# Sums, logits and rows of a pair of heads moved between the score steps of the next pair

## The chip, the cores and the metric

The kernel runs on one core of one Trainium2 chip. The time is the device time of one execution, in microseconds (us); lower is better. The core has five engines that run their own instruction streams in order and meet at semaphores: PE (TensorE; PEld is its weight loads), ACT (ScalarE), DVE (VectorE), POOL (GpSimd) and SP (SyncE, which here only issues DMAs).

## The reference

Two stages. Attention over 4 batches, 8 heads, 768 positions, 64 values per head, in which each query sees only the six best of 24 chunks of keys; then a layer of 8 experts, which takes at most 80 tokens per expert.

```python
k_min, k_max = min and max of k over each chunk of 32 keys
ub = sum over d of maximum(q * k_min, q * k_max), causal by chunk
sel = the 6 chunks with the largest ub, for each query
scores = where(sel & causal, q @ k.T / 8, -1e9)
attn_out = softmax(scores) @ v

x = attn_out as (3072, 512)
logits = x @ w_gate
expert = argmax(logits);  gate = softmax(logits)[expert]
for e in range(8):
    tok = the tokens of expert e; if more than 80, the 80 with the largest gate
    out[tok] = gate[tok] * (relu(x[tok] @ w1[e]) @ w2[e])      # all other rows are 0
```

## The kernel before

A helper, `op(engine, function, r=..., w=...)`, records every operation with what it reads and writes and puts the semaphore waits. Each engine runs its operations in the order in which the program emits them, so the order of the calls below is the order on each engine, and an operation that waits holds up all that its engine has behind it.

Two heads make a pair; 16 pairs (`NP`), four to a batch (`NPB`), are run one after the other. For pair i the loop emits:

- `scores(i)`: six steps. In each, matmuls of keys against queries (L498) and mask matmuls (L504, from `unsT`) fill one of two score tiles `SC[0]`, `SC[1]` in turn; ACT takes the exponential into `EXB` (L509); POOL clears the part above the diagonal (L514, a select) and adds what is there into `ES` (L523, the fold). `ES` becomes the sum over key tiles, from which the softmax's denominators come.
- in the first pair of a batch, `gate`, `gate_digits` and `gate_T` of the batch before: gate values from the logits (DVE, with one exponential on ACT at L586), their transposes on PE into `OB` (L599), and a copy by ACT into the row of candidates `cand` (L601).
- `bounds(i + 1)`: the upper bounds of the next pair (PE into `M0` and `MB`, L463; then DVE to the mask `uns`, L479).
- `transposes(i + 2)`: q and k of the pair after that through `SC[0]` and `SC[1]` (L425), copied out by ACT (qT, rq) and by DVE (kT, and its minima and maxima per chunk); POOL subtracts (L441).
- `load(i + 4)`: q and k by SP.
- `values(i)`: the value products (L534) into `OB`, copied by ACT to `oT` (L538). Then v of pair i + 2 is loaded.
- `unselT(i + 1)`: transposes of the mask (L485) and ACT's copy to `unsT` (L487).
- `wload`: one megabyte of an expert's weights, issued by POOL.
- `rows(i)`: six transposes of `oT` into `OB` (L559).
- `sums(i)`: into `M0`, the pair's part of the logits (`oT` by the gate weights, L544), then the denominators (`ES` by ones, L549); DVE turns them (L552) and takes reciprocals.
- `scale_rows(i)`: DVE scales the rows into `xp` (L567) and the logits into `lgp` (L571), and SP stores `xp` to memory (L573).
- `rounds(i, ..)`: between these, ten rounds per batch (three in each of the first three pairs of the next batch, one in the fourth), each a maximum of 8 over `cand` and a replacement (L620, L622), which find the 80 best tokens of each expert.

After the last pair come the gate of the last batch, its ten rounds, the slots of the tokens, and the experts.

Of the kernel before, what the change touches and what calls it, by code (L numbers as in the profile page):

```python
# [5 lines left out]
ACTF = mybir.ActivationFunctionType  # L6
# [141 lines left out]
def bass_quest_chunk_select__then__topk_capacity_drop_kernel(  # L148
# [10 lines left out]
    B, H, S, D = q.shape  # L159
    E = moe_w_gate.shape[1]  # L160
    Fd = moe_w1.shape[2]
    Dm = moe_w_gate.shape[0]
    CAP = int(moe_capacity)
    NT = S // 128
# [4 lines left out]
    NPB = H // 2  # L169
    NP = B * NPB  # L170
# [4 lines left out]
    def ts(i, n=128):  # L175
        return bass.ts(i, n)
# [27 lines left out]
    with ExitStack() as pers:  # L204
# [16 lines left out]
        op = sy.op  # L221

        with nc.Block() as blk:

            @blk.sync
            def _body(_unused):
# [259 lines left out]
                           r=["uns", "ident_bf"], w=["MB"], inc=(t == NT - 2))  # L486
                    op("act", lambda: ac.activation(unsT[j][:], MB[:, 0:(NT - 1) * 128], ACTF.Copy), r=["MB"], w=[f"unsT{j}"])  # L487

                def scores(i):
                    j = i % 2  # L490
                    for st, pieces in enumerate(STEPS):
                        s = st % 2
                        for pi, (kt, q0, q1, c) in enumerate(pieces):
                            last = pi == len(pieces) - 1
                            for h in range(2):
                                pr = slice(h * 64, h * 64 + 64)
                                o = SC[s][:, h * 512 + c:h * 512 + c + q1 - q0]
                                op("pe", lambda: pe.matmul(o, kT[j][pr, ts(kt)], qT[j][pr, q0:q1], start=True, stop=False),  # L498
                                   r=[f"kT{j}", f"qT{j}"], w=[f"SC{s}"], inc=False)
                            b0 = max(q0, 128)  # L500
                            for h in range(2):
                                pr = slice(h * 64, h * 64 + 64)
                                o = SC[s][:, h * 512 + c + b0 - q0:h * 512 + c + q1 - q0]
                                op("pe", lambda: pe.matmul(o, ind[pr, ts(kt)], unsT[j][pr, b0 - 128:q1 - 128],  # L504
                                                           start=False, stop=True),
                                   r=[f"ind{h}", f"unsT{j}"], w=[f"SC{s}"], inc=last)
                        W = pieces[-1][3] + pieces[-1][2] - pieces[-1][1]
                        src = bass.AP(SC[s], 0, [[1024, 128], [512, 2], [1, W]])
                        op("act", lambda: ac.activation(Ex(st, None, 0, W), src, ACTF.Exp, scale=SCALE),  # L509
                           r=[f"SC{s}"], w=[f"E{st}"])  # L510
                        d = DIAG[st]
                        a = Ex(st, None, d, 128)
                        ad, ak = (ES[:, :, 0:128], "ES0") if st == 0 else (a, f"E{st}")
                        op("gp", lambda: gp.affine_select(ad, a, pattern=[[0, 2], [1, 128]], compare_op=ALU.is_ge, fill=0.0,  # L514
                                                          base=0, channel_multiplier=-1), r=[f"E{st}"], w=[ak])
                        for (s2, c2, q0, q1) in ADDS[st]:
                            n = q1 - q0
                            o = ES[:, :, q0:q1]
                            in1 = Ex(s2, None, c2, n)
                            first = FIRST.get((s2, c2))  # L520
                            in0 = Ex(first[0], None, first[1], n) if first else o
                            kt = [f"ES{t}" for t in range(q0 // 128, q1 // 128)]
                            op("gp", lambda: gp.tensor_tensor(o, in0, in1, ALU.add),  # L523
                               r=[f"E{s2}", f"E{first[0]}"] if first else [f"E{s2}"] + kt, w=kt)
# [32 lines left out]
                def rows(i):  # L557
                    for t in range(NT):
                        op("pe", lambda: pe.transpose(OB[:, ts(t)], oT[:, ts(t)], ident_f[:]),  # L559
                           r=["oT0", "oT1", "ident_f"], w=[f"O{t // 4}"], inc=(t in (3, NT - 1)))  # L560
# [12 lines left out]
                    op("sp", lambda: sp.dma_start(xdst, xp[:]), r=["xp"], w=[f"xd{i}"],  # L573
                       dsem=f"d_xd")

                def gate(b):
                    j0 = b * NT

                    def along(t, n=NT):
                        return bass.AP(t, 0, [[n, 128], [1, n], [0, E]])  # L580

                    op("dve", lambda: ve.tensor_reduce(lg[:], lgp[:], AX, ALU.add),
                       r=[f"lgp{p}" for p in range(NPB)], w=["lg"])
                    op("dve", lambda: ve.tensor_reduce(lmax[:], lg[:], AX, ALU.max), r=["lg"], w=["lmax"])
                    op("dve", lambda: ve.tensor_tensor(lg[:], lg[:], along(lmax), ALU.subtract), r=["lg", "lmax"], w=["lg"])
                    op("act", lambda: ac.activation(lgx[:], lg[:], ACTF.Exp), r=["lg"], w=["lgx"])  # L586
                    op("dve", lambda: ve.scalar_tensor_tensor(oh[:], lg[:], 0.0, rank_c[:], ALU.is_ge, ALU.mult),
                       r=["lg", "rank_c"], w=["oh"])
                    op("dve", lambda: ve.tensor_reduce(lmax[:], oh[:], AX, ALU.max), r=["oh", "lmax"], w=["lmax"])
                    op("dve", lambda: ve.tensor_reduce(lsum[:], lgx[:], AX, ALU.add), r=["lgx"], w=["lsum"])  # L590
                    op("dve", lambda: ve.tensor_tensor(oh[:], oh[:], along(lmax), ALU.is_equal), r=["oh", "lmax"], w=["oh"])
                    op("dve", lambda: ve.tensor_scalar(lsum[:], lsum[:], 1e-9, None, ALU.add), r=["lsum"], w=["lsum"])
                    op("dve", lambda: ve.reciprocal(gt6[:], lsum[:]), r=["lsum"], w=["gt6"])
                    op("dve", lambda: ve.tensor_tensor(gv[:, j0:j0 + NT, :], oh[:], along(gt6), ALU.mult),  # L594
                       r=["oh", "gt6"], w=[f"gv{b}"])

                def gate_T(b):
                    for t in range(NT):
                        op("pe", lambda: pe.transpose(OB[0:E, ts(t)], gv[:, b * NT + t, :], ident_f[:]),  # L599
                           r=[f"gv{b}", "ident_f"], w=["O0" if t < 4 else "O1"], inc=(t in (3, NT - 1)))  # L600
                    op("act", lambda: ac.activation(cand[:, CAP:CAP + S], OB[0:E, 0:S], ACTF.Copy), r=["O0", "O1"], w=["cand"])  # L601

                def gate_digits(b):

# [22 lines left out]

                ROUNDS = CAP // 8

                def rounds(i, lo, hi):  # L630

                    if i < NPB:
                        return
                    for n in range(lo, hi):
                        m = (i % NPB) * 3 + n
                        if m < ROUNDS:
                            top_round(m, False)

                def warm(n):
                    for _ in range(n):  # L640
# [17 lines left out]
                    pr = slice(h * 64, h * 64 + 64)  # L658
                    op("dve", lambda: ve.tensor_copy(wg[pr, :, h * E:(h + 1) * E], wgr[pr, :, :]), r=["wg", f"wgr{h}"], w=[f"wg{h}"])
                for i in range(NP):  # L660
                    scores(i)
                    if i % NPB == 0 and i:
                        gate(i // NPB - 1)
                        gate_digits(i // NPB - 1)
                    if i % NPB == 0 and i:
                        gate_T(i // NPB - 1)
                    if i + 1 < NP:
                        bounds(i + 1)
                    if i + 2 < NP:
                        transposes(i + 2)  # L670
                    if i + 4 < NP:
                        load(i + 4, "qk")
                    rounds(i, 0, 1)
                    values(i)
                    if i + 2 < NP:
                        load(i + 2, "v")
                    if i + 1 < NP:
                        unselT(i + 1)
                    rounds(i, 1, 2)
                    if i < NP - 1:  # L680
                        wload(i // 2, i % 2)
                    rows(i)
                    sums(i)
                    scale_rows(i)
                    rounds(i, 2, 3)
                    if i % 3 == 2 and i < 12:
                        zk = f"w1_{E - 1}"
                        zr = bass.AP(w1s[E - 1], 0, [[DB * Fd, 128], [1, 2 * Dm]])
                        if i == 2:
                            op("dve", lambda: ve.memset(zr, 0.0), w=[zk])  # L690
                        g = i // 3
                        zs = bass.AP(w1s[E - 1], 0, [[DB * Fd, 128], [0, NT], [1, 2 * Dm]]).bitcast(F32)
                        zd = bass.AP(out.tensor, out.offset + g * NT * 128 * Dm, [[Dm, 128], [128 * Dm, NT], [1, Dm]])
                        op("sp", lambda: sp.dma_start(zd, zs), r=[zk], w=[f"outz{g}"], dsem=f"d_zero{g}")


                b = B - 1
                gate(b)
                gate_T(b)
                gate_digits(b)  # L700
# [152 lines left out]
```

## Time and profile before

| | |
|---|---|
| time, median of 3 runs | 373.32 us (371.21 to 375.81) |
| time of the profiled execution | 370.24 us |
| its span, first to last instruction | 368.5 us |
| PE busy | 297.6 us, 81% |
| POOL busy | 231.8 us, 63% |
| DVE busy | 231.2 us, 63% |
| ACT busy | 149.3 us, 41% |
| granted TensorE clock, mean | 0.915 |

Busy time is summed over a span that has different stages: 16 pairs of heads up to about 295 us, then some 40 us in which DVE is nearly alone, then the experts. What an engine's share means has to be read from one stage. Ends of matmuls are modelled. The granted clock is a share of 2.4 GHz.

### The profile page before, as it was taken

How to read it: one execution, taken by the hardware profiler on the slowest of the kernel's cores; microseconds unless marked ns; L12 is line 12 of the kernel's file. 1: busy time of each engine (PE TensorE's matmuls, PEld its weight loads, DVE VectorE, ACT ScalarE, POOL GpSimd, SP SyncE). 2: the span in 40 equal slices, each digit the busy share in tenths (PEclk: the TensorE clock that was granted, in tenths of full speed). 3: DMA queues.
4: the chain of work that ended last, by engine and by line, in shares of the span. 5: the costliest groups of instructions: out<-in, count | busy, mean ns of one | idle time of the engine just before them, and what ended most of it. 6: DMA issues, size and time to landing. Idle time of an engine off the chain costs nothing.

```text
span 368.5 us, 7857 instructions
## 1 busy us (share of the span) xinstructions
PE 297.6 (81%) x3244; PEld 183.4 (50%) x3244; DVE 231.2 (63%) x591; ACT 149.3 (41%) x202; POOL 231.8 (63%) x313
## 2 busy tenths in 40 slices
PE   6599999997899999969999999699989610034993
PEld 6255656463656465536556564456454400024771
DVE  3734425254987696759896963896866079881442
ACT  3273645545345536353736455345535110002320
POOL 5077869696739696785778696919696940006422
PEclk9699999999899999999999999899999855555999
DMA  9937889899495999786989778763638090001211
GB/s 175 193 67 137 159 143 177 138 299 171 91 156 114 143 305 165 143 126 129 265 189 181 136 156 131 221 104 77 114 67 133 4 135 1 0 2 42 59 55 53
DMA packets 104964, 47.50 MB, mean 129 GB/s; under 512 B 88955, under 2 KB 97269, under 8 KB 104928
## 3 DMA queue, kind: packets, MB, share of 16 engines
q1 hardware_dynamic: 89920, 27.94, 32.5%
q0 software_dynamic: 13440, 18.67, 31.8%
q10 hardware_dynamic: 1568, 0.39, 0.6%
q8 instruction: 25, 0.41, 0.4%
q14 instruction: 11, 0.09, 0.1%
HBM read 53.10 MB, written 10.75 MB: 173 GB/s over the span
## 4 chain that ended last, share of the span: by engine, by line
POOL 40%; PE 34%; issue 12%; ACT 7%; DVE 4%; DMA 1%; POOLq 0%
POOL ES L523 32%; PE SC L498 10%; ACT EXB L509 7%; POOL EXB L514 6%; PE OB L534 5%; PE OB L797 4%; PE M L549 4%; PE SC L782 3%; PE SC L504 2%; PE SC L425 2%; PE M L463 1%; PE OB L559 1%; DVE gv L594 1%; DMA kn<-x_rows,idx 1%; PE OB L599 1%
## 5 line engine op out<-in xcount | busy, mean ns | idle before, releaser
L509 ACT ACTIVATE EXB<-SC 128x1024 f32<-128x1024 f32 x96 | 86.3, 916 | 60.9 <-PE SC L504 58.9
L523 POOL TENSOR_TENSOR ES<-ES,EXB 128x256 f32<-128x256 f32 (+1 forms) x112 | 106.8, 965 | 6.4
L498 PE MATMUL SC<-qT,kT 64*128 64x512 f32 (+3 forms) x512 | 98.0, 471 | 1.8
L534 PE MATMUL OB<-EXB,vn 128*64 128x256 f32 (+2 forms) x704 | 71.9, 360 | 0.0
L498 PEld LDWEIGHTS SC<-qT,kT 64*128 64x128 f32 x512 | 40.9, 188 | 42.4 <-ACT EXB L509 26.4
L534 PEld LDWEIGHTS OB<-EXB,vn 128*64 128x64 f32 x704 | 46.7, 137 | 23.0 <-issue 10.0
L523 POOL TENSOR_TENSOR ES<-EXB 128x768 f32<-128x768 f32 (+1 forms) x32 | 49.3, 1541 | 1.3
L620 DVE MAX8 top<-cand 8x8 f32<-8x848 f32 (+1 forms) x40 | 40.2, 1006 | 1.9 <-ACT cand L601 1.3
L504 PE MATMUL SC<-unsT,ind 64*128 64x384 bf16 (+3 forms) x256 | 38.9, 297 | 0.0
L514 POOL TENSOR_SCALAR_AFFINE_SELECT EXB<-EXB 128x256 f32<-128x256 f32 x80 | 31.0, 407 | 10.7 <-ACT EXB L509 10.7
L538 ACT ACTIVATE oT<-OB 128x512 f32<-128x512 f32 (+1 forms) x32 | 15.7, 490 | 53.5 <-PE OB L534 53.5
L622 DVE MATCH_REPLACE8 cand<-top,cand 8x848 f32<-8x848 f32 (+1 forms) x36 | 35.7, 992 | 0.0
L467 DVE STREAM_TRANSPOSE M<-M 128x160 f32<-128x160 f32 x16 | 5.8, 363 | 46.3 <-PE MB L463 46.3
L514 POOL TENSOR_SCALAR_AFFINE_SELECT ES<-EXB 128x256 f32<-128x256 f32 x16 | 6.4, 400 | 43.2 <-ACT EXB L509 43.2
L552 DVE STREAM_TRANSPOSE M<-M 128x192 f32<-128x192 f32 x16 | 6.3, 393 | 35.8 <-PE M L549 35.8
L763 POOL DMA_INDIRECT qn<-x_rows,idx x4 | 3.9, 980 | 35.4 <-issue 35.4
L504 PEld LDWEIGHTS SC<-unsT,ind 64*128 64x128 bf16 x256 | 13.0, 95 | 14.4 <-issue 11.1
L430 ACT ACTIVATE qT<-SC 128x768 f32<-128x768 f32 x16 | 13.0, 811 | 17.2 <-PE SC L425 17.2
L549 PE MATMUL M<-ES,onc 128*32 128x192 f32 x256 | 14.3, 343 | 5.0 <-POOL ES L523 4.3
L774 ACT ACTIVATE rq<-MB 128x320 bf16<-128x320 bf16 x4 | 1.7, 437 | 39.5 <-PE MB L771 39.5
L425 PE MATMUL SC<-ident_f,qn 128*128 128x128 f32 x96 | 15.1, 298 | 3.1 <-ACT EXB L509 1.4
L714 PE MATMUL M<-dg,ones 8*128 8x8 f32 x2 | 0.6, 367 | 20.9 <-DVE dg L712 20.9
(141 smaller groups left out, 449.8 us busy)
## 6 DMA issues: line engine op xcount, KB each, us to landing
w1s<-in_moe_w_dram POOLq DMA_DIRECT2D x8, 1024.0 KB, 9.6
w2s<-in_moe_w_dram POOLq DMA_DIRECT2D x7, 1024.0 KB, 10.3
qn<-in_q_dram SPq DMA_DIRECT2D x32, 192.0 KB, 4.0
vn<-in_v_dram SPq DMA_DIRECT2D x32, 192.0 KB, 3.1
out_dram<-w1s SPq DMA_DIRECT2D x4, 1536.0 KB, 11.5
kn<-in_k_dram SPq DMA_DIRECT2D x30, 192.0 KB, 4.1
x_rows<-xp SPq DMA_DIRECT2D x16, 192.0 KB, 7.5
EXB<-in_moe_w_dram POOLq DMA_DIRECT2D x1, 1024.0 KB, 9.9
```

The lines of the kernel that those rows point to most:

```text
L425: op("pe", lambda: pe.transpose(SC[ps][:, ts(t)], a, ident_f[:]), r=[f"{nm}{s}0", f"{nm}{s}1", "ident_f"], w=[f"SC{ps}"], inc=(t == NT - 1))
L498: op("pe", lambda: pe.matmul(o, kT[j][pr, ts(kt)], qT[j][pr, q0:q1], start=True, stop=False), r=[f"kT{j}", f"qT{j}"], w=[f"SC{s}"], inc=False)
L504: op("pe", lambda: pe.matmul(o, ind[pr, ts(kt)], unsT[j][pr, b0 - 128:q1 - 128], start=False, stop=True), r=[f"ind{h}", f"unsT{j}"], w=[f" ...
L509: op("act", lambda: ac.activation(Ex(st, None, 0, W), src, ACTF.Exp, scale=SCALE), r=[f"SC{s}"], w=[f"E{st}"])
L514: op("gp", lambda: gp.affine_select(ad, a, pattern=[[0, 2], [1, 128]], compare_op=ALU.is_ge, fill=0.0, base=0, channel_multiplier=-1), r=[ ...
L523: op("gp", lambda: gp.tensor_tensor(o, in0, in1, ALU.add), r=[f"E{s2}", f"E{first[0]}"] if first else [f"E{s2}"] + kt, w=kt)
L534: op("pe", lambda: pe.matmul(OB[pr, q0:q1], vn[s][:, kt, h, :], ex, start=(n == 0), stop=last), r=[f"vn{s}{h}", "ES0" if st is None else f ...
L538: op("act", lambda: ac.activation(oT[:, q0:q1], OB[:, q0:q1], ACTF.Copy), r=[f"O{bk}"], w=[f"oT{bk}"])
L549: op("pe", lambda: pe.matmul(M0[c * 32:c * 32 + 32, 0:192], onc[:, h, :], stripes(ES, h * S + c * 32, 0, 0, None), start=False, stop=(h == ...
L620: op("dve", lambda: ve.max(dst, cv), r=["cand"], w=[f"top{int(last)}{n}"])
L622: op("dve", lambda: ve.match_replace(cv, dst, cv, -2.0), r=["cand", f"top{int(last)}{n}"], w=["cand"])
L797: op("pe", lambda: pe.matmul(o, hTv(e)[:, fb * CAP:(fb + 1) * CAP], w2v(e)[:, fb, :], start=(fb == 0), stop=(fb == FB - 1)), r=[f"hT{s}{fb ...
```

## The change

`scores` is split by a range of steps, and the selects and folds of steps 0 and 1 become a function of their own, `folds`. In pair i, steps 0 and 1 come first, then `sums(i - 1)`, then the folds of steps 0 and 1, steps 2 and 3, `rows(i - 1)` and `scale_rows(i - 1)`, and steps 4 and 5. The gate is cut in two: `gate_in` (logits summed, less their maximum, and the exponential) comes after the scores and ahead of `bounds(i + 1)`; the rest and `gate_digits` after it. `gate_T` writes `SC[0]` in place of `OB` and comes after `unselT`. The rounds shift: in the first pair of a batch one at its end, in the other three pairs three each. After the last pair `sums`, `rows` and `scale_rows` of that pair are emitted before the gate.

```diff
--- before.py
+++ after.py
@@ -486,9 +486,9 @@
                            r=["uns", "ident_bf"], w=["MB"], inc=(t == NT - 2))
                     op("act", lambda: ac.activation(unsT[j][:], MB[:, 0:(NT - 1) * 128], ACTF.Copy), r=["MB"], w=[f"unsT{j}"])
 
-                def scores(i):
+                def scores(i, lo, hi):
                     j = i % 2
-                    for st, pieces in enumerate(STEPS):
+                    for st, pieces in list(enumerate(STEPS))[lo:hi]:
                         s = st % 2
                         for pi, (kt, q0, q1, c) in enumerate(pieces):
                             last = pi == len(pieces) - 1
@@ -508,6 +508,11 @@
                         src = bass.AP(SC[s], 0, [[1024, 128], [512, 2], [1, W]])
                         op("act", lambda: ac.activation(Ex(st, None, 0, W), src, ACTF.Exp, scale=SCALE),
                            r=[f"SC{s}"], w=[f"E{st}"])
+                        if lo:
+                            folds(st)
+
+                def folds(*sts):
+                    for st in sts:
                         d = DIAG[st]
                         a = Ex(st, None, d, 128)
                         ad, ak = (ES[:, :, 0:128], "ES0") if st == 0 else (a, f"E{st}")
@@ -573,17 +578,18 @@
                     op("sp", lambda: sp.dma_start(xdst, xp[:]), r=["xp"], w=[f"xd{i}"],
                        dsem=f"d_xd")
 
-                def gate(b):
-                    j0 = b * NT
-
-                    def along(t, n=NT):
-                        return bass.AP(t, 0, [[n, 128], [1, n], [0, E]])
-
+                def along(t, n=NT):
+                    return bass.AP(t, 0, [[n, 128], [1, n], [0, E]])
+
+                def gate_in(b):
                     op("dve", lambda: ve.tensor_reduce(lg[:], lgp[:], AX, ALU.add),
                        r=[f"lgp{p}" for p in range(NPB)], w=["lg"])
                     op("dve", lambda: ve.tensor_reduce(lmax[:], lg[:], AX, ALU.max), r=["lg"], w=["lmax"])
                     op("dve", lambda: ve.tensor_tensor(lg[:], lg[:], along(lmax), ALU.subtract), r=["lg", "lmax"], w=["lg"])
                     op("act", lambda: ac.activation(lgx[:], lg[:], ACTF.Exp), r=["lg"], w=["lgx"])
+
+                def gate(b):
+                    j0 = b * NT
                     op("dve", lambda: ve.scalar_tensor_tensor(oh[:], lg[:], 0.0, rank_c[:], ALU.is_ge, ALU.mult),
                        r=["lg", "rank_c"], w=["oh"])
                     op("dve", lambda: ve.tensor_reduce(lmax[:], oh[:], AX, ALU.max), r=["oh", "lmax"], w=["lmax"])
@@ -596,9 +602,9 @@
 
                 def gate_T(b):
                     for t in range(NT):
-                        op("pe", lambda: pe.transpose(OB[0:E, ts(t)], gv[:, b * NT + t, :], ident_f[:]),
-                           r=[f"gv{b}", "ident_f"], w=["O0" if t < 4 else "O1"], inc=(t in (3, NT - 1)))
-                    op("act", lambda: ac.activation(cand[:, CAP:CAP + S], OB[0:E, 0:S], ACTF.Copy), r=["O0", "O1"], w=["cand"])
+                        op("pe", lambda: pe.transpose(SC[0][0:E, ts(t)], gv[:, b * NT + t, :], ident_f[:]),
+                           r=[f"gv{b}", "ident_f"], w=["SC0"], inc=(t == NT - 1))
+                    op("act", lambda: ac.activation(cand[:, CAP:CAP + S], SC[0][0:E, 0:S], ACTF.Copy), r=["SC0"], w=["cand"])
 
                 def gate_digits(b):
 
@@ -627,14 +633,14 @@
 
                 ROUNDS = CAP // 8
 
-                def rounds(i, lo, hi):
+                def rounds(i, m):
 
                     if i < NPB:
                         return
-                    for n in range(lo, hi):
-                        m = (i % NPB) * 3 + n
-                        if m < ROUNDS:
-                            top_round(m, False)
+                    k = i % NPB
+                    n = 0 if m == 2 and k == 0 else 3 * k - 2 + m
+                    if k or m == 2:
+                        top_round(n, False)
 
                 def warm(n):
                     for _ in range(n):
@@ -658,31 +664,39 @@
                     pr = slice(h * 64, h * 64 + 64)
                     op("dve", lambda: ve.tensor_copy(wg[pr, :, h * E:(h + 1) * E], wgr[pr, :, :]), r=["wg", f"wgr{h}"], w=[f"wg{h}"])
                 for i in range(NP):
-                    scores(i)
-                    if i % NPB == 0 and i:
+                    scores(i, 0, 2)
+                    if i:
+                        sums(i - 1)
+                    folds(0, 1)
+                    scores(i, 2, 4)
+                    if i:
+                        rows(i - 1)
+                        scale_rows(i - 1)
+                    scores(i, 4, 6)
+                    first = i % NPB == 0 and i > 0
+                    if first:
+                        gate_in(i // NPB - 1)
+                    if i + 1 < NP:
+                        bounds(i + 1)
+                    if first:
                         gate(i // NPB - 1)
                         gate_digits(i // NPB - 1)
-                    if i % NPB == 0 and i:
-                        gate_T(i // NPB - 1)
-                    if i + 1 < NP:
-                        bounds(i + 1)
                     if i + 2 < NP:
                         transposes(i + 2)
                     if i + 4 < NP:
                         load(i + 4, "qk")
-                    rounds(i, 0, 1)
+                    rounds(i, 0)
                     values(i)
                     if i + 2 < NP:
                         load(i + 2, "v")
                     if i + 1 < NP:
                         unselT(i + 1)
-                    rounds(i, 1, 2)
+                    if first:
+                        gate_T(i // NPB - 1)
+                    rounds(i, 1)
                     if i < NP - 1:
                         wload(i // 2, i % 2)
-                    rows(i)
-                    sums(i)
-                    scale_rows(i)
-                    rounds(i, 2, 3)
+                    rounds(i, 2)
                     if i % 3 == 2 and i < 12:
                         zk = f"w1_{E - 1}"
                         zr = bass.AP(w1s[E - 1], 0, [[DB * Fd, 128], [1, 2 * Dm]])
@@ -695,6 +709,10 @@
 
 
                 b = B - 1
+                sums(NP - 1)
+                rows(NP - 1)
+                scale_rows(NP - 1)
+                gate_in(b)
                 gate(b)
                 gate_T(b)
                 gate_digits(b)
```

## Rows read from the trace of the kernel before

**Rows 1.** Windows cut at pairs' first score matmuls: length, then busy us (instructions) per engine.
```profile
core 0: us, PE busy (x) PEld busy (x) DVE busy (x) ACT busy (x) POOL busy (x), PEclk, DMA share, GB/s
16.80:34.36 17.56, 17.17 (x176) 10.01 (x175) 7.09 (x22) 9.26 (x12) 13.01 (x18) 0.93 0.53 114
...
83.53:105.20 21.67, 18.08 (x186) 11.41 (x182) 16.82 (x44) 9.48 (x13) 13.21 (x18) 0.92 0.72 118
105.20:121.58 16.38, 15.89 (x180) 9.49 (x176) 12.95 (x32) 8.55 (x11) 12.78 (x17) 1.00 0.77 159
...
154.37:174.43 20.06, 16.46 (x185) 10.03 (x182) 15.26 (x42) 9.48 (x13) 13.26 (x18) 1.00 0.67 118
...
223.58:245.20 21.62, 18.02 (x185) 11.26 (x181) 16.77 (x44) 9.48 (x13) 13.24 (x18) 0.92 0.70 144
...
277.95:295.08 17.13, 14.02 (x130) 7.63 (x126) 5.53 (x11) 6.37 (x8) 13.47 (x19) 0.92 0.45 74
```
**Rows 2.** The chain that ended last, one pair: start us, length us, work.
```profile
107.63 1.03 ACT EXB L509
109.21 1.81 POOL ES L523
...
120.79 0.86 PE M L549 x16
```
**Rows 3.** Timeline of one plain pair: start, length, engine, line, [idle before <-releaser].
```profile
107.18 0.38 PE L504 MATMUL SC<-unsT,ind 64*128 64x512 bf16 x2
...
107.63 1.13 PE L498 MATMUL SC<-qT,kT 64*128 64x512 f32 x4
...
108.59 0.38 PE L504 MATMUL SC<-unsT,ind 64*128 64x512 bf16 x2
...
108.81 0.60 PE L498 MATMUL SC<-qT,kT 64*128 64x256 f32 x4
...
109.78 0.28 PE L504 MATMUL SC<-unsT,ind 64*128 64x256 bf16 x2
...
110.12 0.92 PE L498 MATMUL SC<-qT,kT 64*128 64x384 f32 x4
...
111.73 0.32 PE L463 MATMUL M<-qT,kmm 64*32 64x160 f32 x1
...
118.83 0.45 PE L485 MATMUL MB<-ident_bf,uns 128*128 128x128 bf16 x5
...
119.32 0.70 ACT L487 ACTIVATE unsT<-MB 128x640 bf16<-128x640 bf16 x1
...
119.41 0.87 PE L559 MATMUL OB<-ident_f,oT 128*128 128x128 f32 x6
...
120.21 0.53 PE L544 MATMUL M<-oT,wg 128*32 128x192 f32 x8
```
**Rows 4.** Timeline of the last pair, POOL: first fold after step 1, and its next DMA.
```profile
281.47 0.41 POOL L514 TENSOR_SCALAR_AFFINE_SELECT EXB<-EXB 128x256 f32<-128x256 f32 x1 [0.66 <-ACT EXB L509]
...
293.39 0.91 POOL L414 DMA_DIRECT2D EXB<-in_moe_w_dram  x1
```
**Rows 5.** DVE: the products of scale_rows (timeline); a round's maximum (page, costliest groups).
```profile
106.36 0.96 DVE L567 TENSOR_TENSOR xp<-OB,rden 128x768 bf16<-128x768 f32 x1
...
107.23 0.32 DVE L571 TENSOR_TENSOR lgp<-M,rden 128x96 f32<-128x96 f32 x1
...
L620 DVE MAX8 top<-cand 8x8 f32<-8x848 f32 (+1 forms) x40 | 40.2, 1006 | 1.9 <-ACT cand L601 1.3
```
**Rows 6.** Timeline of the first pair of batch 1: the gate.
```profile
91.33 0.20 DVE L590 TENSOR_REDUCE lsum<-lgx 128x6 f32<-128x48 f32 x1 [4.02 <-ACT lgx L586]
...
93.48 0.82 PE L599 MATMUL OB<-ident_f,gv 128*8 128x128 f32 x6 [3.34 <-DVE gv L594]
...
94.34 0.80 ACT L601 ACTIVATE cand<-OB 8x768 f32<-8x768 f32 x1 [3.04 <-PE OB L599]
```
**Rows 7.** Timeline, PE: end of pair 0, and the sums after the last pair.
```profile
31.48 0.45 PE L485 MATMUL MB<-ident_bf,uns 128*128 128x128 bf16 x5
...
293.51 1.51 PE L549 MATMUL M<-ES,onc 128*32 128x192 f32 x16 [2.41 <-POOL ES L523]
```

## The prediction

> **What bounds the kernel now.** I read the windows view first, cut at the first score matmul of each pair [rows 1]. Sixteen pairs of heads follow each other. A plain pair takes 16.38 us; the first pairs of batches 1, 2 and 3 take 21.67, 20.06 and 21.62. Between 34.36 and 277.95 us lie 14 periods: three such first pairs (63.35) and 11 plain ones (180.24, so 16.39 each). In a plain pair PE is busy 15.89 of 16.38, but that hides a loop, which the chain of waits shows [rows 2]: exp on ACT, the fold chain on POOL, the 16 sums matmuls of L549 that need the finished fold, then the next pair's scores and exp. Folds of the next pair can't begin before its exp, its exp not before sums have left PE. So POOL, at 12.8 busy of 16.38, and PE hold each other.
>
> Next I read the PE timeline inside a pair, start against the end before it [rows 3]. Where nothing waits and the tile shape stays, a matmul starts 0.16 before the modelled end of its predecessor (108.81 against 108.59 + 0.38). A later start is a stall:
> - step 2 waits for the exp that frees its bank: 107.63 against 107.56, so 0.07 + 0.16 = 0.23;
> - step 4 likewise: 110.12 against 110.06, 0.22;
> - rows (L559) wait for the copy of oT: 119.41 against 119.28, 0.29;
> - L549 waits for the fold: 120.79 [rows 2] against 120.74, 0.21.
>
> **What is removed in a plain pair.** All four, 0.95 us. Sums of the pair before now stand between steps 1 and 2, rows between 3 and 4, so each exp has other PE work over it; unselT is followed at once by step 0. Its mask matmuls need ACT's copy of unsT, done at 119.32 + 0.70 = 120.02; its first four matmuls take 0.96 (107.63 to 108.59 in step 2) and would run from 119.2 to 120.2, so they cover it. The fold wait goes if POOL is done by then. Counted from step 0 of a pair: steps 0 and 1 end at 2.20 us (107.18 + 0.38 - 0.16 - 105.20), sums' first half adds 0.37, L549 0.79, with one change of shape 3.45, and select 0 starts at about 3.57. The fold chain from select 1 to the weight DMA is 11.92 [rows 4]; with select 0 (0.41) it ends at 15.90. L549 asks for it a period later, after 2.7 us of steps and the first half of sums, at about 18.4. Margin 2.5 us. The small POOL subtract and the weight DMA's issue (0.91) follow the folds and end near 17.1, still before sums. So the loop through POOL is open, and PE's own stream is what is left.
>
> **What is added.** Three more changes of matmul tile shape per pair: nine in place of six. Their price stands in the same timeline: at a bare change the next matmul starts 0.07 before the modelled end of the last (rows 119.41 + 0.87 against sums at 120.21), where the same shape gives 0.16. That is 0.09 each, 0.27 a pair; bounds: 0 below (they may fall on a gap that is there anyway), 0.29 above, the largest of the four stalls. I take 0.09, a direct reading. The Trainium skill (TensorEngine Tiling, Key Properties) says that changing the tiling mode drains TensorE, which speaks against splitting the score steps; the trace agrees that a change costs something. It gives no time.
>
> New wait: bounds(i+1) writes M0, which scale_rows of the pair before now reads only after step 3. Behind it on PE stand transposes and values. From the end of rows, xp takes 0.96 and the logits product 0.32 behind it [rows 5], with latencies about 1.3; PE spends 1.61 on steps 4 and 5 (110.12 to 111.73) [rows 3]. So PE comes 0.3 later than DVE: no cost, if DVE is free. It carries 12.95 in a pair with three rounds [rows 1], a round being 1.0 us for the maximum [rows 5] and, an estimate, as much for the replacement over the same values, so it has 2.8 us to spare in 15.7. The store of xp goes out on SP ahead of the q and k loads of that pair, which wait for the transposes anyway; cost nothing, and half a DMA landing if that cover fails, against two pairs of prefetch.
>
> So a plain pair goes 16.39 - 0.95 + 0.27 = 15.71, a gain of 0.68; over 11 pairs **-7.5 us**.
>
> **First pairs.** Now the gate's chain stands bare on PE [rows 6]: DVE waits 4.02 for the exp of the gate, which sits on ACT behind six score exps; then gv, then PE sits 3.34 us until gate_T, then bounds, transposes and values. In the window the granted clock reads 0.92, and 1.00 in plain pairs [rows 1]: part of it ran at the lower of 1.2 and 2.4 GHz after that idle stretch. The change starts the gate's input before bounds, lets bounds' DVE work cover its exp, and moves gate_T behind values, so the 3.34 and the slow stretch go. What remains: six transposes, 0.82, and a new wait, step 0 of the next pair behind the 0.80 copy out of SC0 [rows 6], with two hand-overs 0.1: **1.72**. Queued behind it on PE is all of that pair. The DVE load falls from 16.82 by one of the two rounds in that window, to 14.8 of 17.4. First pairs: 15.71 + 1.72 = 17.43; three give 52.3 against 63.35: **-11.1 us**. Bounds for the new idle second: at worst a lower clock for about 1 us of work each, +1 us; at best nothing.
>
> **Ends.** Pair 0 no longer has rows and sums: unselT there ends at 31.48 + 0.45 [rows 7], step 0 follows at 31.9 in place of 34.36: **-2.5**. In the last pair folds begin after the sums of pair 14, so L549 starts at 16.0 from step 0 in place of 15.56 (293.51 [rows 7] less 277.95): **+0.5**. After the last sums, rows now follow them at the lower clock (L549 took 1.51 there and 0.86 in a plain pair), while the small DVE steps take 0.9; xp is some 0.5 later (0 to 0.7): **+0.5**. Two more rounds of the batch before fall into pair 15: 4 us of DVE, which is busy 5.53 of 17.13 there [rows 1], so nothing. The last gate_T writes SC0, which nobody else wants then. The ten last rounds and the experts are as they were.
>
> Sum: -7.5 - 11.1 - 2.5 + 0.5 + 0.5 = -20.1, against the profiled execution's 370.24 (span 368.5 and 1.7 around it): 350.1. The median of the three runs is 373.32, 3.1 above; on that scale it is 353.2. I say 352, between.
>
> **Rivals.**
> 1. *The splits eat the pair's gain.* If each added change costs the 0.29 bound rather than 0.09, three cost 0.87 of 0.95; the pair stays at 16.3, first pairs at 18.0, and the sum is -0.9 - 9.3 - 1.5 = -11.7: 358.5, or 361.6 on the median's scale. The rule on drains cited above would lead here if a drain were that long. For: PE's weight loads can't run ahead over a change. Against: the 0.07 readings.
> 2. *First pairs keep a chain.* DVE there now does gate input, bounds, gate, digits, and only then the copy of kT that frees SC1 for step 1 of the next pair. 14.8 of DVE work in 17.4 says it fits; the order within the pair I can't place to better than 1 us. If the copy is 1 to 2 us late in each, three pairs lose 3 to 6: 355 to 358.
> 3. *Slower: DVE becomes the loop.* Rounds of the pair before stand ahead of sums' DVE steps. If these come late, lgp is late, bounds wait for M0, and with bounds come transposes, and with them kT's copy, the reductions and the rounds: a closed ring on DVE. Its work is 12.95, with 1 us of hand-overs (an estimate) 14. It decides from 15.7; from 16.4 plain pairs are slower than now, and to undo 20 us in the 9 pairs with rounds it has to reach 18. No row speaks for 4 us more of DVE work; price at that point 373 and above.
> 4. *The loop stays closed.* If sums still wait for POOL, plain pairs keep 16.39, first pairs take 18.1 (54.3 for 63.35), and 370.24 - 9.1 - 1.5 gives 359.6. It needs the 2.5 us margin gone.
>
> **Numbers.** Forecast 0.62 (own range 346 to 356: drains free and all else right 347, clock loss in first pairs and half of rival 2 above); rival 1 0.16, rival 2 0.14, rival 4 0.04, rival 3 0.04. The range of 345 to 360 holds the forecast, rival 2 and half of rival 1. A measurement of this kernel tells about 2 per cent from no change, 366 on the median's scale. Forecast and rival 2 are under it, rivals 1 and 4 mostly: faster 0.91, within 0.06, slower 0.03.
>
> **What would show it.** Plain pairs of 15.7 from step 0 to step 0; no wait of L549 for POOL except in the last pair; steps 2 and 4 without wait for exp; select 0 released by L549 and no longer by ACT; first pairs of 17.4 with the granted clock at 1.00 and a wait of step 0 for the copy of cand. Wrong it would be with bounds waiting for the lgp product, step 1 after a first pair waiting for kT, or gaps over 0.2 at each change of shape.

## The result and the profile after

The changed kernel takes 348.18 us (median of 4 runs, 347.47 to 348.83) against 373.61 (4 runs, 371.21 to 375.81) before: ratio 0.932, 95% interval 0.926 to 0.938. Its profiled execution took 347.47 with a span of 345.7, that of before 370.24 and 368.5: 22.8 us less. The account below goes by these two executions; by the medians the gain is 25.4, since the runs of the kernel before lie up to 5.6 us above its profiled one.

The windows view of the changed kernel, cut as before at each pair's first score matmul (length; busy us of PE, PEld, DVE, ACT, POOL; granted clock; DMA):

```profile
core 0: us, PE busy (x) PEld busy (x) DVE busy (x) ACT busy (x) POOL busy (x), PEclk, DMA share, GB/s
16.27:31.97 15.70, 15.58 (x146) 9.04 (x146) 7.10 (x22) 8.45 (x11) 10.51 (x14) 0.87 0.48 106
31.97:47.58 15.61, 15.51 (x178) 9.68 (x176) 6.80 (x22) 8.57 (x12) 13.62 (x19) 1.00 0.80 155
78.79:96.07 17.28, 16.20 (x183) 10.13 (x181) 10.88 (x36) 10.25 (x15) 14.05 (x19) 1.00 0.88 165
...
111.74:127.41 15.67, 15.47 (x178) 9.68 (x176) 12.99 (x32) 8.57 (x12) 12.99 (x18) 1.00 1.05 228
...
240.30:254.27 13.97, 13.97 (x166) 8.38 (x164) 11.29 (x30) 7.05 (x10) 11.36 (x17) 1.00 0.71 119
254.27:271.31 17.04, 13.69 (x137) 7.70 (x135) 10.94 (x19) 7.18 (x10) 15.34 (x20) 1.00 0.42 74
```

Against [rows 1]: a plain pair 15.6 to 15.67 in place of 16.39, all three first pairs 17.28 in place of 21.67, 20.06 and 21.62, at a granted clock of 1.00 where it was 0.92, 1.00 and 0.92. Of the others pair 14 has shrunk most, from 16.37 to 13.97; the last pair has become longer, 17.04 from its step 0 to its sums where it was 15.56. With the end of pair 0 (31.97 for 34.36) and what follows the last sums (74.39 for 74.99) the account closes:

| | predicted | measured |
|---|---|---|
| ten plain pairs | -6.8 | -7.4 |
| pair 14 (counted as an eleventh) | -0.7 | -2.4 |
| three first pairs | -11.1 | -11.5 |
| end of pair 0 | -2.5 | -2.4 |
| last pair | +0.5 | +1.5 |
| behind the last sums | +0.5 | -0.6 |
| sum | -20.1 | -22.8 |

The row behind the last sums is within what one kernel scatters there: the changed kernel, run again below, took 76.0 us in that stretch for the 74.4 here.

The PE timeline of a plain pair of the changed kernel (start, length, line; L549 and L554 are now the two halves of sums, L564 rows):

```profile
111.74 1.13 PE L498 MATMUL SC<-qT,kT 64*128 64x512 f32 x4
...
112.70 0.33 PE L504 MATMUL SC<-unsT,ind 64*128 64x384 bf16 x2
...
112.86 1.02 PE L498 MATMUL SC<-qT,kT 64*128 64x512 f32 x4
...
113.72 0.38 PE L504 MATMUL SC<-unsT,ind 64*128 64x512 bf16 x2
...
114.03 0.53 PE L549 MATMUL M<-oT,wg 128*32 128x192 f32 x8
...
114.38 0.83 PE L554 MATMUL M<-ES,onc 128*32 128x192 f32 x16
...
115.15 1.13 PE L498 MATMUL SC<-qT,kT 64*128 64x512 f32 x4
...
117.30 0.28 PE L504 MATMUL SC<-unsT,ind 64*128 64x256 bf16 x2
...
117.51 0.87 PE L564 MATMUL OB<-ident_f,oT 128*128 128x128 f32 x6
...
118.31 0.92 PE L498 MATMUL SC<-qT,kT 64*128 64x384 f32 x4
...
127.02 0.45 PE L485 MATMUL MB<-ident_bf,uns 128*128 128x128 bf16 x5
...
127.41 1.13 PE L498 MATMUL SC<-qT,kT 64*128 64x512 f32 x4
```

Set side by side with [rows 2, 3], from start to start: step 1's mask matmuls to what follows them 0.31 (it was 0.45, to step 2), the halves of sums 0.35 apart (0.58), step 3's to what follows 0.21 (0.34), unselT to what follows 0.39 (0.58). That is 0.14 + 0.23 + 0.13 + 0.19, 0.69 of the 0.72 gained in this pair. Nothing else in it moved by more than 0.02.

The waits view of the changed kernel (who waited for whom: us in total, times, longest):

```profile
POOL ES L519 <- PE M L554: 16.3, 12, 1.6
...
PEld M L554 <- POOL ES L528: 3.6, 2, 3.2
PEld SC L498 <- ACT cand L607: 3.5, 3, 1.2
```

Select 0 is now released by the sums and not by ACT; the sums wait for POOL twice, at pairs 14 and 15; and in the three first pairs the next step 0 waits for the copy out of SC0, as forecast. The first of these, on PE's timeline:

```profile
96.07 1.13 PE L498 MATMUL SC<-qT,kT 64*128 64x512 f32 x4 [0.89 <-ACT cand L607]
```

### The profile page after: what moved, and what is told of

It reads as the page before. It is cut to its first block, busy times and chain, and to the rows that moved or that the text cites. A ratio compares the mean times of both kernels' runs of the same rounds, so it can differ in the third digit from the quotient of the medians.

```text
span 345.7 us, 7895 instructions
## 1 busy us (share of the span) xinstructions
PE 288.7 (83%) x3244; PEld 183.4 (53%) x3244; DVE 232.9 (67%) x591; ACT 149.3 (43%) x202; POOL 231.2 (67%) x313
## 4 chain that ended last, share of the span: by engine, by line
PE 73%; issue 12%; ACT 6%; POOL 4%; DVE 3%; DMA 1%; POOLq 0%; DVEq 0%
PE SC L498 23%; PE OB L539 20%; PE SC L425 6%; PE SC L504 5%; ACT EXB L509 5%; PE OB L815 4%; PE OB L564 3%; PE M L554 3%; PE SC L800 3%; PE M L549 2%; POOL ES L528 2%; PE MB L485 2%; DMA kn<-x_rows,idx 1%; ACT cand L607 1%; ACT unsT L487 1%
## 5 line engine op out<-in xcount | busy, mean ns | idle before, releaser
L498 PEld LDWEIGHTS SC<-qT,kT 64*128 64x128 f32 x512 | 42.4, 189 | 26.5 <-issue 15.5
L572 DVE TENSOR_TENSOR xp<-OB,rden 128x768 bf16<-128x768 f32 x16 | 15.3, 958 | 24.4 <-PE OB L564 24.3
L821 POOL DMA_INDIRECT out_dram<-EXB,idx x8 | 7.4, 920 | 14.6 <-DVE EXB L819 14.6
```

Source lines behind the costliest of these rows:

```text
L572: op("dve", lambda: ve.tensor_tensor(xo, xi, rx, ALU.mult), r=["O0", "O1", "rden"], w=["xp"])
```

## Experiments

Where no number of runs is given, a time is that of one execution. In the first four runs what follows the last sums, where none of them changes any work, took 80.4 to 82.1 us in place of the 74.4 to 75.0 above; the kernel before, run once beside them, took 378.92 us. PE stood 2.2 to 2.7 us in the expert stage of these four for nothing that the profile shows, which no other run has; the rest of the difference is open. All four whole times lie above their expected ranges. So runs are compared by the windows of their pairs and by the pair stage, from the span's start to the last sums: 293.51 us before, 271.31 changed.

**Only the gate's part.** Sums, rows and scaling stand at the end of their pair again:

```diff
-    scores(i, 0, 2); sums(i - 1); folds(0, 1); scores(i, 2, 4)
-    rows(i - 1); scale_rows(i - 1); scores(i, 4, 6)
+    scores(i, 0, 2); folds(0, 1); scores(i, 2, 6)
...
+    rows(i); sums(i); scale_rows(i)        # behind wload
```

> Only the gate's part of the change; sums, rows and the scaling of a pair stand at its end again, as in the kernel before. Theory (a closed loop through POOL sets plain pairs, the bare gate chain sets first pairs): plain pairs back to 16.4 us, also pair 14; first pairs 16.7 to 17.3, since rows and sums now cover the copy out of SC0; profiled time 357 to 360. Rival (plain pairs are set by PE's own stalls at the score banks, the fold does not matter): the same 16.4. Rival (the two parts need each other: without the split the gate still stands bare): first pairs 19 to 21, time 364 to 370.

Measured: 363.0 us, pair stage 279.22. The windows of a first pair and of pair 14:

```profile
83.11:99.55 16.44, 16.12 (x186) 10.02 (x182) 11.69 (x36) 9.44 (x13) 12.18 (x16) 1.00 0.90 162
...
247.25:263.64 16.39, 14.39 (x167) 8.20 (x163) 10.36 (x29) 7.05 (x9) 12.88 (x17) 1.00 0.51 79
```

Plain pairs are back at 16.4, and pair 14 with them, though it has 1.5 us less work for PE (no transposes): that is the loop through POOL, not PE's load. The rival of PE's stalls forecast the same 16.4 for plain pairs; pair 14 tells the two apart. First pairs come out below the 16.7 to 17.3 expected: at 16.44 the gate is nearly free. The likely reason is that in a pair that waits for POOL the six transposes fill time that PE has left over, and rows and sums cover the copy. The gate's part alone is worth 14.3 us of the pair stage.

**Only the move of sums and rows.** The gate as a block ahead of bounds, in OB:

```diff
-    gate_in(b); bounds(i + 1); gate(b); gate_digits(b)      # gate_T behind unselT, in SC[0]
+    gate_in(b); gate(b); gate_digits(b); gate_T(b); bounds(i + 1)      # gate_T in OB
```

> Only sums, logits and rows between the score steps; gate input, gate, digits and gate_T stand together after the scores and ahead of bounds, gate_T in OB, as in the kernel before. Theory: plain pairs 15.66 and pair 14 13.97 as in the changed kernel; first pairs 20 to 22, because PE waits some 4 us for gv and then transposes 0.82; profiled time 357 to 362. Rival (the first pairs gained from the move and not from the gate's new place): first pairs near 17.2, time 348.

Measured: 368.53 us, pair stage 286.35. Two of its three first pairs:

```profile
78.59:100.66 22.07, 17.80 (x183) 11.06 (x182) 15.65 (x41) 9.48 (x14) 14.98 (x21) 0.92 0.67 122
...
216.50:239.67 23.17, 18.90 (x183) 11.77 (x182) 20.45 (x47) 9.48 (x14) 14.93 (x21) 0.85 0.64 141
```

In the first of them gate_T waits for the gate's values, and after the last pair the sums run so:

```profile
91.12 1.14 PE L605 MATMUL OB<-ident_f,gv 128*8 128x128 f32 x6 [4.28 <-DVE gv L600]
...
286.35 1.51 PE L554 MATMUL M<-ES,onc 128*32 128x192 f32 x16 [2.82 <-POOL ES L528]
```

Plain pairs have the 15.6 to 15.67 of the changed kernel; first pairs are 22.07, 21.84 and 23.17, longer than before the change, with the lower clock back. DVE does not wait for the gate's exp here; gate_T waits for the gate's own steps on DVE. So the two parts do different things: 7.2 us by this one, 14.3 by the other, 22.2 together.

**Sums ahead of step 0.** The same work with the loop closed:

```diff
-    scores(i, 0, 2)
     sums(i - 1)
+    scores(i, 0, 2)
```

> As the changed kernel, but the sums of the pair before stand ahead of step 0 in place of behind step 1. The stream of PE is the same but for its order. Theory (loop through POOL: fold, sums, step 0, exp, fold): the loop closes again, plain pairs 16.4 to 17.1, pair 14 too, sums wait for POOL in every pair; 356 to 365. Rival (PE's own stream sets the pair, its stalls for exp and oT were all that the change removed): plain pairs 15.5 to 15.9, 345 to 351.

Measured: 365.56 us, pair stage 283.41. A first pair, and the plain one after it:

```profile
84.43:101.09 16.66, 16.40 (x185) 9.94 (x181) 11.23 (x36) 9.45 (x13) 12.24 (x16) 1.00 0.80 144
101.09:117.74 16.65, 15.82 (x179) 9.49 (x176) 14.51 (x34) 8.56 (x11) 13.77 (x19) 1.00 0.79 148
```
```profile
116.95 0.86 PE L554 MATMUL M<-ES,onc 128*32 128x192 f32 x16 [0.44 <-POOL ES L528]
```

Pairs 1 to 14 take 16.62 to 16.66 each, first pairs and pair 14 too, and the sums of every pair wait for POOL (the second fence shows those of the plain pair). One call moved by two score steps costs 1 us a pair: the loop is what set plain pairs, and the two steps ahead of the sums are what opens it. The rival, PE's stream alone, falls.

**Two more changes of shape.** The logits half of sums between steps 0 and 1:

```diff
-    scores(i, 0, 2); sums(i - 1)
+    scores(i, 0, 1); logits(i - 1); scores(i, 1, 2); sums(i - 1)
```

> As the changed kernel, but the logits half of sums (L549) stands alone between steps 0 and 1: two more changes of the matmul's tile shape per pair, no other work. Theory (0.09 us a change): plain pairs 15.84, time 350 to 351. Rival (a change costs up to 0.29): plain pairs 16.2, time 356.

Measured: 358.79 us, pair stage 276.35. A plain pair, and the start of it (the mask matmuls of step 0, the logits, step 1):

```profile
113.62:129.62 16.00, 15.80 (x177) 9.51 (x175) 12.97 (x32) 8.55 (x12) 12.97 (x18) 1.00 1.05 226
```
```profile
114.58 0.33 PE L504 MATMUL SC<-unsT,ind 64*128 64x384 bf16 x2
...
114.84 0.53 PE L549 MATMUL M<-oT,wg 128*32 128x192 f32 x8
...
115.30 1.13 PE L498 MATMUL SC<-qT,kT 64*128 64x512 f32 x4
...
116.27 0.38 PE L504 MATMUL SC<-unsT,ind 64*128 64x512 bf16 x2
```

16.00 for 15.67, and 15.95 for 15.61 in the early pairs: 0.34 for two changes, 0.17 each. Neither figure was right. The two hand-overs, to the logits and from them, take 0.26 and 0.46 from start to start; in the changed kernel the same starts without a change lie 0.16 (112.70 to 112.86) and 0.35 (114.03 to 114.38) apart, so they cost 0.10 and 0.11. The trace shows a second part of the price, another 0.11: behind a change the four matmuls of a step take 0.97 to their mask matmuls (115.30 to 116.27), where in the changed kernel step 1, which follows step 0 without one, takes 0.86 (112.86 to 113.72). A step that has stalled pays that too: step 2 of the kernel before, which waited for its exp, took 0.96 [rows 3].

**gate_T in OB**, at its new place:

```diff
-    pe.transpose(SC[0][0:E, ts(t)], gv[...], ident_f[:])
+    pe.transpose(OB[0:E, ts(t)], gv[...], ident_f[:])
```

> As the changed kernel, but gate_T writes OB, as in the kernel before, at its new place behind unselT: step 0 of the next pair no longer shares a tile with it. Theory (of the 1.6 us that first pairs take over plain ones, 0.8 are the transposes and 0.9 the wait of step 0 for the copy out of SC0): first pairs 16.4 to 16.5, three of them 2.6 us in all. Rival (the copy costs the same elsewhere, since rows and the next exps stand behind it on ACT and OB): first pairs stay at 17.2, or the pair behind them grows by as much.

Measured: 348.15 us, pair stage 270.61. The pair behind a first pair, and its step 1:

```profile
95.00:111.44 16.44, 15.74 (x176) 9.62 (x175) 13.92 (x34) 8.65 (x12) 12.34 (x17) 1.00 0.78 149
```
```profile
96.80 1.13 PE L498 MATMUL SC<-qT,kT 64*128 64x512 f32 x4 [0.50 <-DVE kT L437]
```

First pairs fall from 17.28 to 16.32, as the theory had it, and the pair behind them rises from 15.67 to 16.44: 0.2 gained of 1.0. The rival had the place right and not the reason: it is DVE's late copy of kT that now holds step 1, which the wait for SC0 had hidden.

**Rows behind bounds:**

```diff
-    rows(i - 1); scale_rows(i - 1); scores(i, 4, 6); bounds(i + 1)
+    scale_logits(i - 1); scores(i, 4, 6)
+    bounds_pe(i + 1); rows(i - 1); scale_rows(i - 1); bounds_dve(i + 1)
```

> As the changed kernel, but rows stand behind bounds and ahead of the transposes, the logits product ahead of the rows' product (after the last pair the gate's input too). Step 4 waits for its exp again (+0.13 net of two changes of shape), and rows cover the 0.4 us in which the transposes wait for the exp that frees SC0. Theory: plain pairs 15.4 to 15.5; the last pair's folds no longer wait for exps that rows had pushed back, so its sums come some 0.7 sooner, 16.3 behind its step 0. Rival (DVE, whose steps all move back by 0.7, becomes late for values or for bounds): plain pairs 15.7 or more.

Measured: 345.79 us, pair stage 268.62. A plain pair and pair 14:

```profile
95.10:110.51 15.41, 15.35 (x176) 9.70 (x176) 11.69 (x29) 7.75 (x10) 12.21 (x17) 1.00 0.68 134
...
237.20:252.51 15.31, 14.11 (x166) 8.82 (x164) 12.84 (x32) 7.07 (x10) 12.93 (x17) 1.00 0.68 109
```
```profile
247.43 0.44 PE L542 MATMUL OB<-ES,vn 128*64 128x128 f32 x4 [1.14 <-DVE xp L582]
```

Plain pairs take 15.41, as expected; the last pair's sums come 16.11 behind its step 0, 0.2 sooner than expected. Pair 14 loses 1.3 of what it had gained, which was not expected. The second fence shows what holds it: its values write OB, which DVE's product of the rows still reads, and in this pair no transposes stand between rows and values to cover that.

**Both edits together.**

> Both edits together: gate_T in OB and rows behind bounds. Theory: they add up, plain pairs 15.4 to 15.5, first pairs 16.2 to 16.3; from the first step of pair 1 to the last sums some 6 us less than in the changed kernel, 341 to 343 where the expert stage is as in its profile. Rival (first pairs are late on DVE, with rows' product ahead of bounds and the gate behind it, and step 1 behind them waits for kT): first pairs plus the pair behind them no shorter than in the changed kernel, 344 to 347.

Measured: 344.89 us (4 runs), ratio to the kernel before 0.927, 0.919 to 0.935; pair stage 267.80. Plain pairs 15.41, first pairs 16.15 to 16.18, the pair behind each of them 16.06. Pairs are as long as the theory had it, and the whole is not: from the first step of pair 1 to the last sums this kernel takes 3.4 us less than the changed one (235.95 for 239.34), where some 6 was expected, and the time lies in the rival's range. The pair behind each first pair is 0.65 longer than a plain one, as the rival had it, with a wait of step 1 for kT; pair 14 is 1.3 longer, as in the run before. A first pair and the one behind it together are 0.7 shorter than in the changed kernel, which the rival had excluded.

**The gate in one piece**, ahead of bounds, with gate_T where the change has it:

```diff
-    gate_in(b); bounds(i + 1); gate(b); gate_digits(b)
+    gate_in(b); gate(b); gate_digits(b); bounds(i + 1)
```

> As the changed kernel, but the gate's input is not split off: input, gate and digits stand together ahead of bounds; gate_T stays behind values. Theory (the split lets bounds' DVE work cover the gate's exp): DVE waits 1 to 1.5 us for that exp, uns comes late and unselT waits for it, kT later still; first pairs 18.5 to 20. Rival (only the place of gate_T mattered; values cover all DVE work): first pairs 17.3 as in the changed kernel.

Measured: 364.38 us, pair stage 287.16. The first pair's window, and in it the gate's exp, DVE's sum behind it, a fold on POOL, the next but one step of DVE, and unselT on PE:

```profile
78.74:99.04 20.30, 16.27 (x183) 10.12 (x181) 13.90 (x38) 10.29 (x15) 14.04 (x19) 0.99 0.80 152
```
```profile
87.92 0.24 ACT L589 ACTIVATE lgx<-lg 128x48 f32<-128x48 f32 x1
...
88.20 0.20 DVE L596 TENSOR_REDUCE lsum<-lgx 128x6 f32<-128x48 f32 x1
...
88.56 1.27 POOL L528 TENSOR_TENSOR ES<-EXB 128x512 f32<-128x512 f32 x1
...
88.58 1.28 DVE L598 TENSOR_SCALAR lsum<-lsum 128x6 f32<-128x6 f32 x1
...
97.05 0.45 PE L485 MATMUL MB<-ident_bf,uns 128*128 128x128 bf16 x5 [2.95 <-DVE uns L479]
```

First pairs of 20.3, 20.31 and 21.21, a little over what was expected, and 1.5 to 2.9 more in the pair behind each, which runs in part at the lower clock (granted 0.84 to 0.91 in these windows; 1.00 in the changed kernel). The cost is there, the reason given for it is not: the sum that needs the exp has no wait in front of it. What holds PE is the order on DVE. Gate and digits occupy it from 87.72 to 94.78, and bounds' steps, with the mask that unselT needs, come behind them.

**Digits behind the transposes**, in the kernel with both edits:

```diff
-    gate(b); gate_digits(b); transposes(i + 2)
+    gate(b); transposes(i + 2); gate_digits(b)
```

> As the kernel with both edits, but the gate's digits (2 us of DVE) stand behind the transposes, so that DVE copies kT before them. Theory (with the wait for SC0 gone, step 1 behind a first pair waits for kT): the pair behind a first pair falls from 16.06 to 15.41, 2 us in all; 342.5 to 343.5. Rival (the lateness moves to the bounds or the reductions behind it): no change, 345.

Measured: 343.03 us (6 runs), ratio 0.924, 0.920 to 0.929; pair stage 266.28. The first pair and the one behind it:

```profile
78.48:94.64 16.16, 16.10 (x183) 10.11 (x181) 9.45 (x30) 9.44 (x14) 13.68 (x18) 1.00 1.02 177
94.64:110.05 15.41, 15.35 (x176) 9.68 (x175) 12.13 (x35) 8.60 (x12) 12.21 (x17) 1.00 0.77 147
```

The pair behind falls to 15.41. A first pair is now 0.75 to 0.78 longer than a plain one, about the six transposes of gate_T (0.82).

**The changed kernel again**, beside it on the same chip:

> The changed kernel itself, on the same chip as the run beside it, so that the two can be compared. Theory and rival alike: 347 to 349, pairs as in its profile; what differs from chip to chip is the expert stage.

Measured: 348.73 us (6 runs), ratio 0.941, 0.936 to 0.946; pair stage 271.11, pairs as in its profile. The expectation puts the difference in the expert stage on the chip. The runs speak against the chip alone: the first four runs, with 80.4 to 82.1 us behind the last sums, and the four with 75.4 to 76.0 ran on one chip. The last version is 5.7 us faster than the changed kernel, 1.6 per cent.

## Why the prediction was right, and where it was off

**Plain pairs.** Shown. The loop through POOL set them, and two score steps ahead of the sums open it: closing it again with the rest of the change in place gives 16.65, leaving it closed gives 16.4 whatever PE has to do. The four stalls and the three changes of shape came out as costed, 0.68 forecast and 0.74 measured. POOL's margin was 1.5 us and not 2.5: in a plain pair the folds end 16.8 from step 0, and not 15.9, and the sums ask for them at 18.3. The prediction left out a wait of 0.70 on POOL for the exp of step 4, which rows now push back; nothing hung on it here. The line, from the plain pair that starts at 111.74:

```profile
122.90 5.61 POOL L528 TENSOR_TENSOR ES<-ES,EXB 128x512 f32<-128x512 f32 x6
```

The 0.09 for a change was, though, the price of a change that takes the place of a stall. One where nothing stalled costs 0.17, as the added splits showed. The forecast's sum held because a stall also pays the slower start of the step behind it (0.96 in step 2, stalled before and behind a change now), so that part cancelled. The prediction had not seen this part, so here it was lucky. The Trainium skill (TensorEngine Tiling (Array Packing), Key Properties) says that a change of the tiling mode drains TensorE. The trace agrees that a change costs time, 0.17 us on average; what the engine does in it no run shows. Rival 1, with 0.29 each, falls.

**Pair 14.** The largest miss: the prediction counted 11 plain pairs, and pair 14 has no transposes. Its window in the kernel before:

```profile
261.58:277.95 16.37, 14.39 (x167) 8.20 (x163) 10.37 (x29) 7.04 (x9) 12.87 (x17) 1.00 0.50 79
```

With 14.39 us of PE work, and held by the loop, it took as long as the others; with the loop open it falls to 13.97. That is 1.7 of the 2.7 us by which the sum was short.

**First pairs.** The term was 1.72 over a plain pair; it is 1.61 to 1.67: 0.8 for the transposes and the wait for the copy out of SC0, 0.89 in the trace. The reason that the gate moved off the path was half right. The split of the gate is not what takes away DVE's wait for the exp (4.02 in [rows 6]): DVE doesn't wait for it with the gate in one piece either. The rows are now scaled behind step 3, so the gate's input comes late; in the run with the gate in one piece its exp starts at 87.92, right behind the score exps, and DVE's next two steps cover it. In the run with only the move, too, DVE doesn't wait for it. What counts is that bounds' steps come first on DVE, and gate_T behind values; the gate in one piece costs 3.0 to 3.9 us in each first pair and 1.5 to 2.9 in the pair behind it, the latter in part through the clock. And rival 2's mechanism was there all along, hidden: kT's copy is late behind a first pair, 0.5 us of wait on PE as soon as the wait for SC0 goes.

**The ends.** The term for pair 0 was right, both small ones were off. The last pair was to cost 0.5 and cost 1.5; its lines, timeline of the changed kernel:

```profile
258.15 0.40 POOL L519 TENSOR_SCALAR_AFFINE_SELECT ES<-EXB 128x256 f32<-128x256 f32 x1 [0.36 <-PE M L554]
...
263.58 0.77 POOL L519 TENSOR_SCALAR_AFFINE_SELECT EXB<-EXB 128x256 f32<-128x256 f32 x2 [0.71 <-ACT EXB L509]
...
271.31 0.86 PE L554 MATMUL M<-ES,onc 128*32 128x192 f32 x16 [2.82 <-POOL ES L528]
...
272.09 0.87 PE L564 MATMUL OB<-ident_f,oT 128*128 128x128 f32 x6
```

Select 0 starts 3.88 from step 0 (254.27), 0.3 later than reckoned, since behind the short pair 14 the sums do wait for POOL; and the fold chain has a new wait of 0.71 for the exp of step 4, which rows between steps 3 and 4 push back. In plain pairs that hides in POOL's margin. With rows behind bounds the last pair's sums come 0.9 sooner, which shows it. Behind the last sums the +0.5 rested on the lower clock, and L554 and rows ran at the higher one, 0.86 and 0.87 for the 1.51 of [rows 7]. That is chance: in the run with only the move the same sums, behind the same wait of 2.82, ran at half speed.

**The number.** The forecast of 352 is 3.8 us over the measured 348.18. Of this 2.7 is the sum, 1.1 of which stands in the row behind the last sums and is no more than scatter. The rest is the 1.9 that was added to come nearer the median of the kernel before; the median of the changed kernel lies only 0.7 above its profiled execution.

**Rivals 3 and 4.** DVE did not close a ring: in plain pairs no wait of bounds for M0 is in the trace. Sums wait for POOL only at the end.

## What to carry to other kernels

An engine that is 97 per cent busy can still be held by a loop through another one; look for a pair or tile with less work that takes just as long, and put independent work of the next round between the last step of the loop and its first. When a wait is removed, ask which later one it was hiding: here the copy out of SC0 hid kT's copy. With rows behind bounds, taking away the first wait gave 0.3 us per first pair and the one behind it, taking away both gave 1.0. Splitting a run of matmuls cost less here than the stall that it replaced (0.09 us a change against 0.2 to 0.3), and about 0.17 us a change of tile shape where nothing stalled.

## What the runs showed of the hardware

A change of tile shape costs in two places: the next matmul starts 0.09 to 0.11 us later against its predecessor's end, and a score step behind it takes 0.11 longer (0.97 for 0.86 to its mask matmuls). The weight loads of the kernel before show where they differ:

```profile
105.20 0.30 PEld L498 LDWEIGHTS SC<-qT,kT 64*128 64x128 f32 x4 [0.30 <-issue]
...
106.16 0.36 PEld L498 LDWEIGHTS SC<-qT,kT 64*128 64x128 f32 x4 [0.33 <-DVE rden L553]
...
107.63 0.30 PEld L498 LDWEIGHTS SC<-qT,kT 64*128 64x128 f32 x4 [0.77 <-ACT EXB L509]
```

Step 1, without a change or a stall ahead of it, has its first load at 106.16, 0.16 ahead of its first matmul (106.32). Behind a change (step 0, 105.20) and behind a stall (step 2, 107.63) the first load and the first matmul start together.

Small DVE steps slow down greatly beside POOL's folds: the sum's correction over 128x6 values took 1.28 us in the run with the gate in one piece. It began and ended with a fold on POOL (88.56 to 89.83). After the last pair, with only POOL's memsets beside it, the changed kernel's timeline has the same line so:

```profile
276.09 0.36 DVE L598 TENSOR_SCALAR lsum<-lsum 128x6 f32<-128x6 f32 x1
```

Not every step slows: in the first pair of the changed kernel, with folds beside them, L593 over 128x48 values took 1.30 us and the two reductions behind it 0.20 and 0.19. The Trainium skill (SBUF — State Buffer, Who interferes with whom) says that a DVE instruction in a two-port mode and GpSimd lock a shared pair of ports against each other for whole instructions, and that tensor_scalar can enter such a mode. The trace fits that, with the 1.28 that end where the fold ends. Whether this step ran in such a mode, and whether the lock is the cause, no run here measured by itself.

The granted clock after a wait is not told by the wait's length alone: the sums of the last pair ran at half speed (granted 0.50) after 2.41 us of idle PE before the change, and at full speed (1.00) after 2.82 behind it. In the run with only the move they ran at half speed after the same 2.82.
